# Another split of a weight load over the DMA engines in a decode block (attention with a KV cache beside a gMLP)

## The chip, the cores and the metric

One Trainium2 chip, one core of it. The metric is the device time of one execution of the kernel in microseconds (us), as the median of several runs. Beside it there is one execution under the hardware profiler; its time and its span are given below, and all durations in this document come from such profiled executions.

## The reference

Four tokens (batch B = 4, one position each, D = 640) go through a layernorm and then through two blocks whose results are added to the input.

```python
xn = _layernorm(x)
# A: attention of one query against a cache, H = 32 heads, Sk = 4096 keys, Dh = 128
q = (xn @ wq)                                   # 640 x 4096
scores = einsum('bhqd,bhkd->bhqk', q, k_cache) * Dh ** -0.5
p = softmax(scores);  o = einsum('bhqk,bhkd->bhqd', p, v_cache);  A = o @ wo
# B: gMLP, Fh = 864
z = gelu(xn @ w_in)                             # 640 x 1728
z1, z2 = z[..., :Fh], _layernorm(z[..., Fh:])
g = w_sp * z2 + b_sp                            # one position, so w_sp is 1 x 1
B = (z1 * g) @ w_out                            # w_out is 864 x 640
return x + A + B
```

Everything is bf16. The caches are 4 x 32 x 4096 x 128 each, 134 MB of K and 134 MB of V; `wq` and `wo` have 5.2 MB each, `w_in` 2.2 MB, `w_out` 1.1 MB (864 rows of 1280 bytes).

## The kernel before

**Loads.** Nearly all bytes are fetched by SyncE's queue (SP) in one fixed order: `wq` (L119), `w_in` (L122), the first 384 rows of `w_out` (L126, L127), two pieces of its other rows (`load_piece`, L139 and L140), then the cache in units of 8 heads of one batch entry, each 128 partitions x 65,536 bytes (`load_unit`, L174 to L181): K of the four batch entries of head group 0, then V and K in turn, last V of the last group. `wo` comes in four parts of 1280 KB (`load_wo`, L187): one after the last K unit of the second group, and three behind everything else (L570 to L572), the last of them cut into five transfers so that the products with it can start before all of it is there. The cache units lie in one buffer `kv` of five half-unit slots; a unit's load waits until the slot's former reader is done, so SP always has one or two units in the queue ahead of the one in use.

**`w_out`.** The product with `w_out` contracts over its 864 rows in chunks of up to 128 (one row per partition). The first nf = 384 rows are the common rows: `FA` = 3 chunks over all 128 partitions, in `kv`. Two transfers bring them, 256 rows as two rows per partition (L126) and 128 rows as one per partition (L127). The other 480 rows lie in `FR` = 17 further chunks in `w_words`, which fill only some partitions; L128 sets that part of `w_words` to zero first. The table `PC` (L61) says how. An entry `(p0, p1, n, k)` puts n rows into each of the partitions p0 to p1; `load_piece` writes the DRAM side with k as the slowest dimension. The three entries move 20 x 10, 12 x 12 and 8 x 17 rows. The first two are issued on SP, the third on GpSimd (POOL), after a small load `walk` of 14 short rows (L141) on the same queue.

```python
FA = 3
FR = 17
PC = ((0, 20, 10, 5), (32, 44, 12, 3), (60, 68, 17, 2))
```

**gMLP.** `z_ps` (L338, L339) gets the products of xn with the columns of `w_in` that belong to the common rows: per contraction chunk (5) and partition group (4) one matmul for two of the three chunks and one for the third, since the rows of the two transfers lie differently. `zr_ps` (L343) gets the others, one matmul for each partition group that an entry of `PC` touches. ScalarE applies GELU (L349, L357, L360); layernorm and gating run on GpSimd and VectorE over 128 x 32*(FA+FR) elements (L371 to L390); then (FA+FR) x 2 products with `w_out` add to `proj` (L403).

**Attention.** Per K unit eight steps `emit_K`: a 32x32-block transpose on VectorE (L425) and eight matmuls (L436). After a group's four K units a softmax, then four V units (`emit_V`, L509). After the last V unit: selection matmul (L531), `oT` (L534 to L543), the products with the last parts of `wo` (`emit_proj` L555, then L599 to L614), one add (L617) and two output transfers (L620).

Of the kernel before, what the change touches and what calls it, by code (L numbers as in the profile page):

```python
# [16 lines left out]
def kernel(  # L17
# [19 lines left out]
    nc = tc.nc  # L37
    P = 128
# [3 lines left out]
    DC = D // P  # L42
# [9 lines left out]
    NG = H // HG  # L52
# [2 lines left out]
    F2 = B_w_in.shape[1]  # L55
    Fh = F2 // 2
    FA = 3
    FR = 17
    nf = FA * P

    PC = ((0, 20, 10, 5), (32, 44, 12, 3), (60, 68, 17, 2))  # L61
    f_at = [nf]
    for p0, p1, n, _ in PC:
        f_at.append(f_at[-1] + (p1 - p0) * n)
    assert Fh == f_at[-1]
    FC = FA + FR
    NOUT = A_wo.shape[1]
# [18 lines left out]
    def misc_ps(shape, dtype):  # L86
        misc_ctr[0] += 1
        return ps_m.tile(shape, dtype, tag="misc", name=f"misc{misc_ctr[0]}")
# [5 lines left out]
    n_p = (2 * TC + 1) * 16  # L94
    w_words = const.tile([P, max(2 * NKT + n_p, FR * NOUT // 2)], F32, name="w_words")
    kT_t = w_words[:, 0:2 * NKT].rearrange("p (i n) -> p i n", i=2)
    pT_t = w_words[:, 2 * NKT:2 * NKT + n_p].bitcast(BF16).rearrange("p (j r) -> p j r", r=32)

    def at_slot(i, n, off=0):
        return kv[:, i * SL + off:i * SL + off + n]  # L100
# [22 lines left out]

    w_out = at_slot(2, FA * NOUT, n_in).rearrange("p (c n) -> p c n", c=FA)

    nc.sync.dma_start(out=w_out[:, 0:2], in_=B_w_out[0:2 * P, :].rearrange("(p c) n -> p c n", p=P))  # L126
    nc.sync.dma_start(out=w_out[:, 2:3], in_=B_w_out[2 * P:nf, :].rearrange("(p c) n -> p c n", p=P))  # L127
    nc.vector.memset(w_words[:, 0:FR * NOUT // 2], 0.0)  # L128
    w_rest = w_words[:, 0:FR * NOUT // 2].bitcast(BF16).rearrange("p (c n) -> p c n", c=FR)

    def load_piece(eng, t):
        p0, p1, n, k = PC[t]
        return eng.dma_start(out=w_rest[p0:p1, 0:n].rearrange("p c n -> p (c n)"),
                             in_=B_w_out[f_at[t]:f_at[t + 1], :].rearrange("(r i c) n -> i r (c n)", i=k, c=n))
# [39 lines left out]
    def load_unit(item):  # L174
        key, u = item
        g, b = divmod(u, B)
        cache = A_k_cache if key == "k" else A_v_cache
        src = cache[b, g * HG:(g + 1) * HG].rearrange("e (m t) d -> (e m) (t d)", t=T)
        c = cuts.get(item, (0, T))
        for t0, t1 in zip(c[:-1], c[1:]):  # L180
            nc.sync.dma_start(out=unit(item, t0, t1), in_=src[:, t0 * Dh:t1 * Dh])  # L181
# [5 lines left out]
    def load_wo(g, c_cuts=(0, HG)):  # L187
        for c0, c1 in zip(c_cuts[:-1], c_cuts[1:]):
            nc.sync.dma_start(out=wo_t[g][:, c0:c1, :], in_=wo_q[g][:, c0:c1, :])  # L189
# [30 lines left out]
    xnT = const.tile([P, DC, 32], BF16)  # L220
# [43 lines left out]
    for q in range(4):  # L264
        nc.gpsimd.tensor_copy(out=SelE[32 * q:32 * q + 32, :, q % 2, :],
                              in_=b8[32 * q:32 * q + 32, 8:8 + HP, None].to_broadcast((32, HP, P // HG)))
# [10 lines left out]
                          in_=ident_f[:].rearrange("p (q x c) -> p q x c", q=2, c=C2))  # L277
# [12 lines left out]
    for hf in range(NH):  # L290
        nc.tensor.matmul(proj[0:32, 0:NO2], lhsT=ident_bf[:XR, 1 - hf:33 - hf],
                         rhs=x_bf[:, hf * NO2:(hf + 1) * NO2], start=(hf == 0), stop=False)
# [4 lines left out]
    for hf in range(2):  # L297
        for c in range(DC):
            for j in range(NG):
                n0 = j * HG * Dh + hf * 512  # L300
                nc.tensor.matmul(q4_ps[32 * j:32 * j + 32, hf * 512:hf * 512 + 512], lhsT=xnT[:, c, :],  # L301
                                 rhs=wq[:, c, n0:n0 + 512], start=(c == 0), stop=(c == DC - 1))
# [14 lines left out]
    w_z = w_in.rearrange("p c (a f) -> p c a f", a=2)  # L317
    z_ps = misc_ps([P, 2, FA, 32], F32)
# [3 lines left out]
    z_in = [[], [], [], []]  # L322
    for t, (p0, p1, n, k) in enumerate(PC):
        src = w_z[:, :, :, f_at[t]:f_at[t + 1]]
        for q in range(p0 // 32, (p1 - 1) // 32 + 1):
# [5 lines left out]
                src_q = src  # L331
            z_in[q].append((t, x0 - 32 * q, x1 - 32 * q, src_q))
    z_of = [[sum((x1 - x0) * PC[t][2] for t, x0, x1, _ in z[:m]) for m in range(len(z) + 1)] for z in z_in]
    w_z2 = w_z[:, :, :, 0:2 * P].rearrange("p c a (q j i) -> p c q a i j", q=4, j=32)
    w_z1 = w_z[:, :, :, 2 * P:nf].rearrange("p c a (q j) -> p c q a j", q=4)
    for c in range(DC):
        for q in range(4):
            nc.tensor.matmul(z_ps[32 * q:32 * q + 32, :, 0:2], lhsT=xnT[:, c, :], rhs=w_z2[:, c, q], start=(c == 0), stop=False)  # L338
            nc.tensor.matmul(z_ps[32 * q:32 * q + 32, :, 2], lhsT=xnT[:, c, :], rhs=w_z1[:, c, q], start=False,  # L339
                             stop=(c == DC - 1))  # L340
        for q in range(4):
            for m, (_, _, _, src) in enumerate(z_in[q]):
                nc.tensor.matmul(zr_ps[32 * q:32 * q + 32, :, z_of[q][m]:z_of[q][m + 1]], lhsT=xnT[:, c, :], rhs=src[:, c],  # L343
                                 start=(c == 0 and m == 0), stop=(c == DC - 1 and m == len(z_in[q]) - 1))
# [5 lines left out]
    for q in range(4):  # L350
        rows = slice(32 * q, 32 * q + 32)
        for m, (t, x0, x1, _) in enumerate(z_in[q]):
            p0, p1, n, k = PC[t]
            z = zr_ps[rows, :, z_of[q][m]:z_of[q][m + 1]]
# [3 lines left out]
            else:  # L358
                for a in range(2):
                    nc.scalar.activation(out=dst[:, a].rearrange("p c (i r) -> p c i r", i=k),  # L360
                                         in_=z[:, a].rearrange("p (r i c) -> p c i r", i=k, c=n), func=ACT.Gelu_apprx_tanh)
# [36 lines left out]
    for f0 in range(0, FC, 4):  # L398
        for hf in range(NH):
            for fc in range(f0, min(f0 + 4, FC)):  # L400
# [3 lines left out]
                                 rhs=(w_out[:, fc] if fc < FA else w_rest[:, fc - FA])[:, hf * NO2:(hf + 1) * NO2],  # L404
                                 start=(fc == 1 and hf == 0), stop=False)
# [11 lines left out]
    def emit_K(u, k):  # L417

        g, b = divmod(u, B)
        hh = first.get(u, 0) ^ (k // 4)  # L420
        qp, kh = k // 2 % 2, k % 2
        t0 = 2 * TC * (2 * hh + qp)
        kw = unit(("k", u), t0, t0 + 2 * TC).bitcast(F32).rearrange("p (t w) -> p t w", w=KW)[:, :, 32 * kh:32 * kh + 32]
        kT = kT_t[:, k % 2]
        nc.vector.transpose(kT.rearrange("p (t r) -> p t r", r=32), kw)  # L425
        if ("S", g) not in state:
            S_new = ps_s.tile([P, 2, TC, M], F32, tag="S", name="S")
            state[("S", g)] = S_new
        S_ps = state[("S", g)]
        kb = kT.bitcast(BF16).rearrange("p (i t e m w) -> p i t e m w", i=2, e=NE, m=M, w=2)  # L430
        w0 = 8 - (b * C2 + hh)
        for w in range(2):
            for i in range(2):
                for e in range(NE):
                    q = 2 * qp + e
                    nc.tensor.matmul(S_ps[32 * q:32 * q + 32, i], lhsT=QZ[:, b, 2 * kh + w, e, w0:w0 + 32],  # L436
                                     rhs=kb[:, i, :, e, :, w], start=(b == 0 and k < 4 and kh == 0 and w == 0),
                                     stop=(b == B - 1 and k >= 4 and kh == 1 and w == 1))
# [89 lines left out]
    def emit_sel(g):  # L528

        ox = misc_ps([P, B, P // HG, HG], F32)  # L530
        nc.tensor.matmul(ox[:].rearrange("p b q c -> p (b q c)"), lhsT=SelX[:].rearrange("p h q -> p (h q)"),  # L531
                         rhs=state["R"][:].rearrange("p b d -> p (b d)"), start=True, stop=True)
        om = ppool.tile([P, B, P // HG, HG], F32, tag="p", name="om")
        nc.vector.tensor_tensor(out=om[:], in0=ox[:], in1=MkQ[:, None, :, None].to_broadcast((P, B, P // HG, HG)), op=ALU.mult)  # L534
        state[("om", g)] = om
# [19 lines left out]
    def emit_proj(g, h2=range(2), close=False):  # L555
        for h in h2:
            for hf in range(NH):
                for c in range(4 * h, 4 * h + 4):
                    o_mul(proj[32 * (c % 2):32 * (c % 2) + 32], g, c, hf, hf * NO2, (hf + 1) * NO2, False,
                          close and c == HG - 1 and hf == NH - 1)  # L560

    fill_qz(0)
    for i, item in enumerate(seq):
        if i + 1 < len(seq):
            key, u = seq[i + 1]
            load_unit(seq[i + 1])
            if key == "k" and u == 2 * B - 1:
                load_wo(u // B - 1)
        else:
            load_wo(NG - 3)  # L570
            load_wo(NG - 2)
            load_wo(NG - 1, (0, 2, 4, 6, 7, 8))  # L572
        key, u = item
        g, b = divmod(u, B)
        if key == "k":
            done = b == B - 1 and g > 0
            for k in range(8):
                emit_K(u, k)
                if done and k == 1:
                    emit_sel(g - 1)  # L580
                if done and k == 2:
                    emit_oT(g - 1)
                if done and k == 5 and g == 1:
                    emit_proj(g - 1)
            if b == B - 1:
                if g < NG - 1:
                    fill_qz(g + 1)
                softmax(g)
        else:
            emit_V(u)  # L590
# [58 lines left out]
```

## Time and profile before

| | us |
|---|---|
| median of 3 runs (lowest to highest) | 663.54 (663.45 to 664.74) |
| the profiled execution's own time | 663.36 |
| its span, first to last instruction | 661.6 |
| VectorE busy | 377.3 (57%) |
| TensorE busy | 281.7 (43%) |
| ScalarE, GpSimd busy | 73.9, 70.3 |
| bytes moved | 282.60 MB, 427 GB/s over the span |

How to read it: the page gives busy time by engine, DMA queues by packets and bytes, the chain of work that ended last and the costliest groups of instructions. The view by windows gives, for each stretch of time, the busy time of each engine and the DMA share, which is the mean busy share of the core's 16 DMA engines. The trace behind it holds, for every DMA packet, its queue, start, duration and size, and, for every transfer, the moments at which its 16 shares landed (one semaphore step each). From these, times are quoted as "landings", in us from the start of the span.

### The profile page before, as it was taken

What the parts mean: (1) busy time and instruction counts of PE and PEld (TensorE: products, weight loads), DVE (VectorE), ACT (ScalarE), POOL (GpSimd) and SP (SyncE); (2) the same over time, 40 slices, a digit from 0 to 9 for tenths busy, and PEclk for the clock granted to TensorE, in tenths of its full rate; (3) what the DMA queues carried; (4) which work ended last, traced back from release to release, by engine and by line L of the source; (5) the groups of instructions that cost most, each with busy time, mean ns of one, the idle gap of its engine ahead of it and who ended that gap; (6) DMA issues with size and microseconds to landing.
All of it is one profiled execution on the core that took longest, in us unless ns stands there. A gap on an engine that the chain in (4) does not pass through costs nothing.

```text
span 661.6 us, 5513 instructions
## 1 busy us (share of the span) xinstructions
PE 281.7 (43%) x2293; PEld 106.9 (16%) x2293; DVE 377.3 (57%) x307; ACT 73.9 (11%) x143; POOL 70.3 (11%) x138
## 2 busy tenths in 40 slices
PE   0445555437052455334435075532606245652236
PEld 0221111112011121111112021110202112120012
DVE  4329989766191758718346196864629175971112
ACT  0300000330100000340200000070110000043200
POOL 3620000030200000130300000030020000003300
PEclk9868879778687697677759677875867778666779
DMA  8999999999999999999999999999999999999997
GB/s 367 458 421 440 425 436 445 436 421 440 421 436 437 444 405 436 441 441 436 433 420 428 437 422 445 442 425 432 432 433 432 433 440 411 446 432 429 423 423 286
DMA packets 7276, 282.60 MB, mean 427 GB/s; under 512 B 929, under 2 KB 1324, under 8 KB 1836
## 3 DMA queue, kind: packets, MB, share of 16 engines
q1 hardware_dynamic: 7112, 282.07, 98.9%
q8 instruction: 18, 0.29, 0.2%
q0 software_dynamic: 112, 0.18, 0.1%
q14 instruction: 6, 0.05, 0.0%
q10 hardware_dynamic: 28, 0.01, 0.0%
HBM read 282.25 MB, written 0.01 MB: 427 GB/s over the span
## 4 chain that ended last, share of the span: by engine, by line
DMA 74%; DVE 12%; issue 11%; PE 2%; ACT 0%; SPq 0%; DVEq 0%; ACTq 0%
DMA kv<-in_A_k_cache_dram 63%; DVE w_words L425 11%; DMA kv<-in_A_v_cache_dram 5%; DMA kv<-in_A_wo_dram 3%; DMA kv<-in_A_wq_dram 3%; PE O L509 1%; DVE w_words L491 0%; PE S L436 0%; DVE Zb L469 0%; DVE m L443 0%; PE last L552 0%; ACT p_bf L485 0%; SPq L189 0%; PE proj L552 0%; PE misc L447 0%
## 5 line engine op out<-in xcount | busy, mean ns | idle before, releaser
L425 DVE STREAM_TRANSPOSE w_words<-kv 128x2048 f32<-128x2048 f32 x128 | 282.8, 2275 | 127.2 <-DMA kv<-in_A_k_cache_dram 127.2
L436 PE MATMUL S<-w_words,QZ 128*32 128x512 bf16 x1024 | 183.3, 490 | 262.5 <-DVE w_words L425 262.5
L436 PEld LDWEIGHTS <-QZ 128*32 128x32 bf16 x1024 | 59.2, 110 | 384.3 <-issue 318.1
L509 PE MATMUL O<-kv,Zb 128*32 128x512 bf16 x1024 | 72.0, 443 | 57.6 <-DMA kv<-in_A_v_cache_dram 51.1
L473 ACT ACTIVATE Zb<-w_words,MkE 32x128 bf16<-32x128 bf16 x120 | 60.9, 508 | 117.2 <-PE O L509 103.3
L518 DVE TENSOR_TENSOR om<-O,Mk 128x512 f32<-128x512 f32 x15 | 10.4, 692 | 92.1 <-PE O L509 92.1
L471 POOL TENSOR_SCALAR Zb<-w_words,MkE 32x128 bf16<-32x128 bf16 x60 | 43.3, 722 | 138.6 <-PE O L509 118.0
L485 ACT ACTIVATE p_bf<-S,negmax 128x1024 bf16<-128x1024 f32 x4 | 4.5, 1114 | 401.5 <-DVE negmax L453 401.5
L509 PEld LDWEIGHTS <-Zb 128*32 128x32 bf16 x1024 | 33.3, 110 | 96.1 <-issue 66.5
L469 DVE TENSOR_SCALAR Zb<-w_words,MkE 32x128 bf16<-32x128 bf16 x76 | 24.9, 327 | 2.3
L411 POOL COPY QZ<-qT 32x32 bf16<-32x32 bf16 x16 | 5.0, 315 | 184.9 <-PE S L436 184.3
L519 DVE TENSOR_REDUCE R<-om 128x128 f32<-128x512 f32 x15 | 15.3, 1020 | 0.5
L496 POOL TENSOR_SCALAR rs<-MkB,rowsum 128x4 f32<-128x4 f32 x4 | 1.2, 296 | 112.2 <-ACT p_bf L485 112.2
L491 DVE STREAM_TRANSPOSE w_words<-p_bf 128x1024 bf16<-128x1024 bf16 (+1 forms) x8 | 9.6, 1240 | 5.9 <-ACT p_bf L485 4.1
L542 POOL MEMSET oT<- 128x66 bf16 x4 | 0.5, 146 | 98.0 <-PE proj L552 98.0
L443 DVE TENSOR_REDUCE m<-S 128x1 f32<-128x1024 f32 x4 | 4.9, 1224 | 6.1 <-PE S L436 6.1
L521 DVE TENSOR_SCALAR R<-O,Mk 128x128 f32<-128x128 f32 x1 | 0.4, 351 | 13.0 <-PE O L509 13.0
L531 PE MATMUL misc<-R,SelX 128*128 128x512 f32 x8 | 4.5, 644 | 7.2 <-DVE R L519 5.5
L301 PE MATMUL q<-kv,xnT 128*32 128x512 bf16 x40 | 4.5, 631 | 6.4 <-DVE xnT L222 6.4
L498 PE MATMUL misc<-rs,SelE 128*128 128x4 f32 x8 | 2.3, 364 | 10.4 <-POOL rs L496 10.4
L552 PE MATMUL proj<-kv,oT 128*8 128x320 bf16 x52 | 5.6, 352 | 1.2 <-DMA kv<-in_A_wo_dram 1.2
L128 DVE MEMSET w_words<- 128x5440 f32 x1 | 4.6, 4592 | 1.9 <-issue 1.9
(107 smaller groups left out, 87.9 us busy)
## 6 DMA issues: line engine op xcount, KB each, us to landing
kv<-in_A_k_cache_dram SPq DMA_DIRECT2D x8, 4096.0 KB, 30.2
kv<-in_A_v_cache_dram SPq DMA_DIRECT2D x1, 6144.0 KB, 28.6
kv<-in_A_wq_dram SPq DMA_DIRECT2D x1, 5120.0 KB, 17.2
kv<-in_A_wo_dram SPq DMA_DIRECT2D x3, 1280.0 KB
kv<-in_B_w_in_dram SPq DMA_DIRECT2D x1, 2160.0 KB, 22.7
kv<-in_A_v_cache_dram SPq DMA_DIRECT2D x1, 2048.0 KB
kv<-in_A_wo_dram SPq DMA_DIRECT2D x3, 320.0 KB, 22.7
kv<-in_B_w_out_dram SPq DMA_DIRECT2D x1, 320.0 KB, 23.0
```

Source lines behind the costliest of these rows:

```text
L411: nc.gpsimd.tensor_copy(out=QZ[r0:r0 + 32, :, :, :, 8 + 8 * hp], in_=qT[32 * g:32 * g + 32, NE * hp:NE * hp + NE].rearrange("p e a b -> p ...
L425: nc.vector.transpose(kT.rearrange("p (t r) -> p t r", r=32), kw)
L436: nc.tensor.matmul(S_ps[32 * q:32 * q + 32, i], lhsT=QZ[:, b, 2 * kh + w, e, w0:w0 + 32], rhs=kb[:, i, :, e, :, w], start=(b == 0 and k < ...
L443: nc.vector.tensor_reduce(out=m1[:], in_=S_ps[:].rearrange("p i t m -> p (i t m)"), axis=AX.X, op=ALU.max)
L469: nc.vector.tensor_scalar(out=dst, in0=src, scalar1=mk, scalar2=None, op0=ALU.mult)
L471: nc.gpsimd.tensor_scalar(out=dst, in0=src, scalar1=mk, scalar2=None, op0=ALU.mult)
L473: nc.scalar.activation(out=dst, in_=src, func=ACT.Copy, scale=mk)
L491: nc.vector.transpose(pT_t[:, j0:j1, :], blocks)
L509: nc.tensor.matmul(O_ps[32 * q:32 * q + 32, :, :], lhsT=Zb[b % 2][:, w].rearrange("p h c -> p (h c)"), rhs=vv[:, w * 4 * Dh:(w + 1) * 4 * ...
L518: nc.vector.tensor_tensor(out=om4[:], in0=O_ps[:], in1=Mk4[:, :, None].to_broadcast((P, 4, Dh)), op=ALU.mult)
L519: nc.vector.tensor_reduce(out=R, in_=om4[:].rearrange("p c d -> p d c"), axis=AX.X, op=ALU.add)
L552: nc.tensor.matmul(dst[0:nb, 0:n1 - n0], lhsT=state[("oT", g)][:, c0:c0 + nb], rhs=wo_t[g][:, c, n0:n1], start=start, stop=stop)
```

## The change

The rows of `w_out` are dealt out anew. The 384 common rows come in one transfer, three rows to each partition, in place of two transfers. The 480 other rows lie in 15 chunks in place of 17: 20 partitions x 9 rows, 20 x 9 and 8 x 15. The matmuls of `z` for the common rows become one per contraction chunk and partition group. Apart from that, the third part of `wo` (`load_wo(NG - 2)`) is cut into two transfers of 640 KB.

```diff
-    FR = 17
+    FR = 15
     nf = FA * P
 
-    PC = ((0, 20, 10, 5), (32, 44, 12, 3), (60, 68, 17, 2))
+    PC = ((0, 20, 9, 5), (32, 52, 9, 5), (60, 68, 15, 2))
...
-    nc.sync.dma_start(out=w_out[:, 0:2], in_=B_w_out[0:2 * P, :].rearrange("(p c) n -> p c n", p=P))
-    nc.sync.dma_start(out=w_out[:, 2:3], in_=B_w_out[2 * P:nf, :].rearrange("(p c) n -> p c n", p=P))
+    nc.sync.dma_start(out=w_out, in_=B_w_out[0:nf, :].rearrange("(p c) n -> p c n", p=P))
...
-    w_z2 = w_z[:, :, :, 0:2 * P].rearrange("p c a (q j i) -> p c q a i j", q=4, j=32)
-    w_z1 = w_z[:, :, :, 2 * P:nf].rearrange("p c a (q j) -> p c q a j", q=4)
+    w_za = w_z[:, :, :, 0:nf].rearrange("p c a (q j i) -> p c q a i j", q=4, j=32)
     for c in range(DC):
         for q in range(4):
-            nc.tensor.matmul(z_ps[32 * q:32 * q + 32, :, 0:2], lhsT=xnT[:, c, :], rhs=w_z2[:, c, q], start=(c == 0), stop=False)
-            nc.tensor.matmul(z_ps[32 * q:32 * q + 32, :, 2], lhsT=xnT[:, c, :], rhs=w_z1[:, c, q], start=False,
-                             stop=(c == DC - 1))
+            nc.tensor.matmul(z_ps[32 * q:32 * q + 32], lhsT=xnT[:, c, :], rhs=w_za[:, c, q], start=(c == 0), stop=(c == DC - 1))
...
             load_wo(NG - 3)
-            load_wo(NG - 2)
+            load_wo(NG - 2, (0, 4, 8))
             load_wo(NG - 1, (0, 2, 4, 6, 7, 8))
```

In the order of the instructions, the change takes 40 TensorE instructions out of the `z` products and 8 out of the products with `w_out`, one transfer out of SP's list at the start and adds one to it near the end. VectorE, ScalarE and GpSimd keep their number of instructions; those over 640 (5440) elements per partition go over 576 (4800).

## The prediction

> **What bounds the kernel now.** I read the queues and the slices first. The 16 DMA engines are busy in every slice, and nearly all packets are on one queue.
>
> ```profile
> DMA  8999999999999999999999999999999999999997
> ...
> q1 hardware_dynamic: 7112, 282.07, 98.9%
> q8 instruction: 18, 0.29, 0.2%
> q0 software_dynamic: 112, 0.18, 0.1%
> q14 instruction: 6, 0.05, 0.0%
> ```
>
> So no single wait sets the end; the sum of packets does, on the engine that has most. The two "instruction" queues fetch program code through the same engines: 18 packets of 16 KB and six of 8 KB within the span. They matter below.
>
> Next I read the last stretch of the chain of waits.
>
> ```profile
> 633.82 23.04 DMA kv<-in_A_wo_dram
> 656.86 0.04 issue
> 656.91 0.23 PE last L552
> 657.14 0.64 PE proj L552 x4
> 657.78 0.68 PE last L552 x15
> 658.46 0.04 issue
> 658.50 0.32 PE last L552 x4
> 658.82 0.02 issue
> 658.85 0.32 DVE o_bf L617
> ```
>
> The last four matmuls start at 658.50, 0.04 us after the last landing of `wo` (658.46), and TensorE was idle before them. From there a fixed 3.1 us follow (matmuls, add, output transfer) to 661.6. The span is therefore: the last landing on the slowest engine, plus 3.1.
>
> Last, the view by windows, DMA share in the last but one column.
>
> ```profile
> 652.00:655.00 3.00, 2.08 (x18) 0.79 (x18) 1.97 (x3) 0.00 (x0) 0.00 (x0) 1.00 0.97 390
> 655.00:656.50 1.50, 1.19 (x16) 0.76 (x16) 0.00 (x0) 0.00 (x0) 0.00 (x0) 1.00 0.88 328
> 656.50:657.50 1.00, 0.66 (x9) 0.36 (x7) 0.48 (x1) 0.00 (x0) 0.00 (x0) 1.00 0.36 127
> 657.50:658.50 1.00, 0.96 (x21) 0.73 (x17) 0.61 (x2) 0.00 (x0) 0.00 (x0) 1.00 0.11 36
> ```
>
> The engines do not finish together: 0.97 busy, then 0.36, then 0.11. A share that is moved off the last ones is gained; a share put on them is lost, us for us. So the question is which engines are last, and what the new split does to them.
>
> **Who is last.** The page doesn't name the engines, but the 16 landings of every transfer do it indirectly: an engine works through its queue in order, at a constant pace (a 65,536-byte packet takes 2.418 us in nearly all cases), so its distance from the earliest engine changes only where it gets something extra. Sorted distances, in us:
>
> ```
> transfer (earliest landing)   distance of the 16 landings from the earliest
> first K unit (40.60)   0 .13 .14 .17 .29 .32 .36 1.47 1.65 | 2.23 2.28 | 3.62 3.76 | 4.50 4.81 4.92
> K half (89.01)         0 .14 .18 .19 .33 .37 1.44 1.66 1.80 | 2.27 3.21 | 3.62 3.77 | 4.49 4.81 4.92
> V unit (471.06)        0 .09 .22 .28 .43 .82 1.73 1.75 1.89 1.96 2.13 2.28 3.34 3.46 3.69 3.70
> last of wo (654.91)    0 1.43 1.59 1.64 1.66 1.76 1.89 1.91 2.01 2.16 3.12 3.13 3.32 3.37 3.51 3.55
> ```
>
> The groups of the first row follow from the pieces of `w_out`. Piece 1 lands on five engines at 23.23, 23.46, 23.48, 23.50, 23.78; piece 2 on three at 25.50, 25.75, 26.07. Four packets of 15,360 bytes take 4 x 573 ns = 2.29 us, and 23.23, 23.46 and 23.78 plus 2.29 are just these three. So the three of piece 2 are among the five of piece 1 (distances 4.5 to 4.9: the **heavy three**), and the other two of the five are at 2.23 and 2.28 (the **light two**). GpSimd's piece sits on two more (3.62, 3.76).
>
> The Trainium skill, page "DMA: Bandwidth & Descriptors", section "Why a DMA increments its semaphore by 16 and not by 1", says that a transfer from SP over k engines takes the lowest-numbered k. The landings just read agree. By it, the changed second piece, now with k = 5, falls on the very same five.
>
> Now the code fetches. At 88.3 us there is an 8 KB code packet (0.32 us). In the next landings one of the light two has gone from 2.27 to 3.21, +0.94: the engine loses more than the packet's own time. The same engine, call it **X**, gains 0.94 again at 279 (3.22 to 4.16, corrected for the earliest engine, which itself moves by 1.43 on a 16 KB packet at 288) and 0.96 at 469 (2.73 to 3.69). X thus pays about 2.85 us for code. One of the heavy three pays 0.67 at 35 and 0.68 at 279, the other light one 0.67 at 614. The 16 KB packets, some 1.5 us each, go round eight other engines in turn. At the end X, which had the small share, stands beside the heavy three at the top (3.69 and 3.70 at 471).
>
> **The change, part by part.**
>
> 1. *Pieces.* A packet of 9 rows (11,520 bytes) should take 479 - 1280 x 0.0367 = 432 ns (479 ns for 12,800 and 573 for 15,360 bytes give 0.0367 ns a byte). Two pieces of four packets and a 9 ns semaphore packet each: 3.47 us on each of the five. Heavy three before: 4 x 479 + 4 x 573 + 18 ns = 4.23, now **-0.75**. Light two before: 4 x 479 + 9 ns = 1.93, now **+1.55**. GpSimd's two: packets of 19,200 for 21,760 bytes, 4 x 94 ns = -0.38.
> 2. *Common rows.* 8 x (102 + 55) + 18 ns = 1.27 before; 8 packets of 3840 bytes at 102 + 47 = 149 ns and one semaphore, 1.20: -0.07 on all engines.
> 3. *Third part of `wo` in two.* 8 x 385 ns become 16 x 196 (102 + 94), +0.06 and a semaphore: +0.07 on all. Parts 2 and 3 cancel. An earlier start of the products with it gains nothing: the last landing, not TensorE's backlog, starts the last four matmuls.
> 4. *Compute.* L128 shrinks by 12% of 4.59 us (-0.54), TensorE loses 24 matmuls (20 of 0.19 us, overlapped, four of about 0.13), GpSimd's three long steps 10% of 2.5 + 0.9 + 1.5 us. All of it ends by 43.6 us, and the next thing, the first transpose, starts at 45.74 after 7.1 us of waiting for the first K unit. Cost: nothing. If that cover were gone, the gain would be some 1.5 us of compute, but only in front of a stream of loads that has to arrive anyway.
> 5. *Queues.* SP's list loses L127 (0.92 us), but SP waits there for L128 until 6.55. One issue more near the end costs 0.4 us at 633, 15 us and more ahead of the data. As a transfer waits for a semaphore to come free, now the last two of `wo` wait for landings of the last V unit (644.2 and 649.1, later by what X adds); the first engine reaches the last one at 654.5, and the first `wq` packet started 1.0 us after its issue. Covered by about 3 us. The nearest approach elsewhere is the third K unit, issued at 54.76 with the engines busy till 59.95. No idle engine arises.
> 6. *Code.* TensorE has 48 instructions fewer, so its 16 KB packets come a little later, on engines that aren't last (the third round costs at most 1.5 us on one that stands at 1.9 or less). VectorE, ScalarE and GpSimd keep their counts, so I take the 8 KB fetches as unchanged in time, place and cost.
>
> **Sum.** At the last landing X is the one at 3.51 or 3.55; with +1.55 it stands at 5.06 to 5.10 from an earliest engine that stays at 654.91. The heavy three drop to 2.6 to 2.8. The last landing moves from 658.46 to 659.99, +1.5 us, and everything behind it with it. From the profiled execution's 663.36 that is 664.9; the median of the runs shown is 0.18 above that execution. I predict **665.0**, +0.22%. X's packets could take 0.1 less or more each way, as distances shrank by 0.15 over the small packets at the end: 664.6 to 665.3.
>
> The Trainium skill, page "Runtime: NRT & Kernel Launch", section "Instruction fetch mechanics", calls instruction fetch hidden behind the pace at which instructions are issued. For the engines that run the instructions no wait here contradicts it; for the loads the trace does (some 0.95 three times on X). If the rule held for the loads too, the five would carry nothing else and this change would level them.
>
> **Rivals.**
>
> - *X's code goes elsewhere (not slower).* Fetch engines could be laid out anew for the changed program. If none of the two hit hardest is among the light two, these end at 1.43 + 1.55 = 3.0, the heavy three at 2.8, and the last is the engine at 3.13 after its third 16 KB packet: 3.55 - 3.13, -0.4 us, **663.1**. X itself would then stand at 3.53 - 2.85 + 1.55 = 2.2. The break-even lies where X pays 2.85 - 1.53 = 1.3 us for code in place of 2.85: one fetch, not three. For: the placement is seen in one execution only. Against: the instruction counts that drive the 8 KB fetches don't change. The same 663.1 would come if the second piece fell on five other engines. Chance 0.25.
> - *More code on X.* A fourth 8 KB fetch (they came 190 us apart; the next would be near 659) slips in ahead of the end: +0.95, **666.0**. Against: VectorE's counts are the same. Chance 0.07.
> - *Part of X's tail is free.* Alone at the end, X might run faster than the constant pace, or something else is already as late as X: half of 1.5 is lost, **664.2**. Against: small packets take 55 ns and 385 ns in the crowd and near the end. Chance 0.08.
>
> **Chances.** Forecast 0.60, rivals 0.25, 0.07, 0.08. About 0.2%, 1.3 us, is what a measurement can tell from no change here, so 664.87 is the bound. The forecast lies just over it; I give it 0.8 to come out there (0.48), and with the second rival 0.55 for slower. Same: 0.12 + 0.08 + 0.22 = 0.42. Faster by over 1.3 us would need the last landing below a distance of 2.2, where several engines stand that the change doesn't touch: 0.03. The range takes in the first and nearly the second rival: 662.9 to 666.0.
>
> **What would show it.** Right: the last landing near 660.0, the latest alone for about 1.5 us; the DMA share near 0.06 between 658.5 and 659.5; in the first K unit distances of about 3.8 (two), 3.7 to 4.2 (three) in place of 2.25 and 4.5 to 4.9, and one of the two stepping up by 0.95 at 88, 279 and 469. Wrong: the steps fall on another group, or a K or V load starts with an idle engine before it.

## The result and the profile after

| | before | changed |
|---|---|---|
| median of 16 runs (lowest to highest), us | 663.39 (663.25 to 664.74) | 664.78 (664.56 to 664.98) |
| profiled execution, span, us | 661.6 | 662.9 |

The medians lie 1.39 us (0.21%) apart; the ratio over all runs is 1.0019, 95% interval 1.0011 to 1.0026. So the changed kernel is slower, clear of the measurement, and stands right at the 0.2% that the prediction had set as a bound: just over it by the medians, just under it by the ratio. Two of the 16 runs of the kernel before (664.42 and 664.74; beside e1 to e4 below, 11 of 33) came out about 1 us above the rest, which pulls the ratio down and not the medians; no trace here shows why. (663.39 is the median over 16 runs of the kernel before; the prediction knew three.)

The queues on the page of the changed kernel hold the same bytes in sum as before (0.02 MB went from q0, GpSimd's piece, to q1), in ten packets more on q1, and the same code packets:

```profile
q1 hardware_dynamic: 7122, 282.09, 98.7%
q8 instruction: 18, 0.29, 0.2%
q0 software_dynamic: 112, 0.16, 0.1%
q14 instruction: 6, 0.05, 0.0%
```

The end of the chain of waits, changed kernel:

```profile
618.48 31.92 DMA kv<-in_A_v_cache_dram
650.40 0.02 issue
650.42 9.39 DMA kv<-in_A_wo_dram
659.81 0.04 issue
659.85 0.32 PE last L548 x4
660.17 0.02 issue
660.20 0.32 DVE o_bf L613
```

Again the last four matmuls start 0.04 us after the last landing, now at 659.81 in place of 658.46, and again 3.1 us follow. The chain goes through the issue at 650.4, which waited for a semaphore of the last V load; that wait sets nothing, since the earliest engine came to that transfer only at 654.4. The view by windows of the changed kernel shows who is late (DMA share in the last but one column):

```profile
656.50:657.50 1.00, 0.71 (x8) 0.28 (x7) 0.05 (x2) 0.00 (x0) 0.00 (x0) 1.00 0.29 109
657.50:658.50 1.00, 0.48 (x7) 0.46 (x8) 0.47 (x1) 0.00 (x0) 0.00 (x0) 1.00 0.10 38
658.50:659.50 1.00, 0.97 (x19) 0.66 (x18) 0.62 (x2) 0.00 (x0) 0.00 (x0) 1.00 0.06 20
659.50:660.50 1.00, 0.57 (x8) 0.20 (x7) 0.30 (x1) 0.00 (x0) 0.00 (x0) 1.00 0.06 16
```

0.06 is one engine of 16. From 658.5 on a single engine works, and everything waits for it. In the last window part of the share is that engine's last 0.3 us and a code packet. The landings, read as in the prediction:

```
changed kernel, earliest landing   distance of the 16 landings from the earliest
first K unit (40.62)   0 .01 .03 .05 .20 .27 .39 .48 1.24 | 3.11 3.24 | 3.57 3.60 3.73 3.96 4.14
K half (89.04)         0 .04 .06 .19 .27 .49 1.25 1.54 1.93 | 3.09 3.24 | 3.60 3.71 3.95 4.16 4.51
V unit (470.89)        0 .26 .35 .51 .57 1.83 1.86 1.93 2.00 2.23 2.32 2.36 2.67 2.92 3.14 5.22
last of wo (654.80)    0 1.73 1.75 1.82 1.83 1.83 1.89 1.97 2.06 2.24 2.51 2.77 2.85 3.00 3.64 5.01
```

The five engines with 72 rows start together at 3.57 to 4.14. One of them, X, steps from 3.57 to 4.51 at the 8 KB code packet near 89.7 us, again by 0.95 near 279 and from 4.23 to 5.22 at 472. At the end it is alone at 5.01; the next one stands at 3.64.

### The profile page after: what moved, and what is told of

Its sections match the earlier page's. It is cut to its first block, busy times and chain, and to the rows that moved or that the text cites. A ratio compares the mean times of both kernels' runs of the same rounds, so it can differ in the third digit from the quotient of the medians.

```text
span 662.9 us, 5465 instructions
## 1 busy us (share of the span) xinstructions
PE 285.2 (43%) x2269; PEld 108.3 (16%) x2269; DVE 376.7 (57%) x307; ACT 73.9 (11%) x143; POOL 69.2 (10%) x138
## 4 chain that ended last, share of the span: by engine, by line
DMA 76%; DVE 12%; issue 11%; PE 1%; SPq 0%; DVEq 0%
DMA kv<-in_A_k_cache_dram 65%; DVE w_words L421 11%; DMA kv<-in_A_v_cache_dram 9%; DMA kv<-in_A_wo_dram 1%; PE O L505 1%; DVE w_words L127 1%; SPq L132 0%; DVEq L421 0%; SPq L180 0%; PE last L548 0%; DVE o_bf L613 0%
## 5 line engine op out<-in xcount | busy, mean ns | idle before, releaser
L505 PE MATMUL O<-kv,Zb 128*32 128x512 bf16 x1024 | 75.1, 459 | 58.7 <-DMA kv<-in_A_v_cache_dram 40.6
L530 DVE TENSOR_TENSOR om<-misc,h 128x512 f32<-128x512 f32 x4 | 2.8, 691 | 4.9 <-PE misc L527 4.9
```

The source lines that it names most:

```text
L505: nc.tensor.matmul(O_ps[32 * q:32 * q + 32, :, :], lhsT=Zb[b % 2][:, w].rearrange("p h c -> p (h c)"), rhs=vv[:, w * 4 * Dh:(w + 1) * 4 * ...
```

## The experiments

The theory: the end is X's last landing, X is one engine, and it is late because it gets the same rows as four others and VectorE's code besides. All times below are medians; each group was run beside the kernel before on the same chip (663.31 to 663.38).

**The piece table alone, both ways.** `e1_old_pieces` is the changed kernel with

```diff
-    PC = ((0, 20, 9, 5), (32, 52, 9, 5), (60, 68, 15, 2))   # FR = 15
+    PC = ((0, 20, 10, 5), (32, 44, 12, 3), (60, 68, 17, 2)) # FR = 17
```

> The changed kernel with the piece table of before (20 x 10, 12 x 12, 8 x 17 rows, 17 chunks); the common rows stay in one transfer and the third part of wo in two. Theory (the share on engine X sets the end): X has 40 rows again, the last landing goes back by 1.4 to 1.5 us, time 663.3 to 663.5, ratio to before 0.999 to 1.000. Rival (the merged transfer, the cut of wo or the z products cost the time): it stays at 664.6 to 664.9, ratio 1.002.

Measured 663.40, ratio 0.9997 (0.9988 to 1.0006). `e2_new_pieces` is the kernel before with the opposite edit.

> The kernel before with the piece table of the change alone (20 x 9, 20 x 9, 8 x 15 rows, 15 chunks); common rows in two transfers, wo uncut. Theory: X has 72 rows, stands alone 1.4 us behind the next at the end; 664.7 to 665.0, ratio 1.002. Rival (the cost is in the other edits): 663.3 to 663.5, ratio 1.000.

Measured 664.85, ratio 1.0018 (1.0009 to 1.0027). The end of the chain of waits in e1:

```profile
649.39 9.44 DMA kv<-in_A_wo_dram
658.83 0.04 issue
658.87 0.32 PE last L548 x4
```

So the piece table brings the whole loss. The merged transfer of the common rows, the cut in `wo` and the fewer `z` products together change nothing that can be measured.

**Which of the five X is.** `e3_four_engines` gives four engines 80 rows and the fifth 40; `e4_four_engines_less` gives them 76 and 32.

```diff
+    PC = ((0, 20, 10, 5), (32, 48, 10, 4), (60, 68, 15, 2))  # e3, FR = 15
+    PC = ((0, 20, 8, 5), (32, 48, 11, 4), (60, 68, 18, 2))   # e4, FR = 18
```

> The changed kernel with 20 x 10, 16 x 10 (k = 4) and 8 x 15 rows: four engines get 80 rows, the fifth of the five 40. It asks which of the five X is. If X is the fifth: X is back at its 40 rows (distance of the last landing 3.5), the other light one goes to 3.35, the heavy three to 3.0 to 3.2; 663.3 to 663.5, ratio 0.999 to 1.000, though each of four engines has 8 rows more than in the change. If X is the fourth: X at 3.53 + 1.92 = 5.45, 665.1 to 665.4, ratio 1.003. Rival that the engine with most rows is last, wherever code goes (72 in the change, 80 here, 88 before): time between the two, nearer to before only if more rows on four engines were good, which it can't explain.

> The changed kernel with 20 x 8, 16 x 11 (k = 4) and 8 x 18 rows, 18 chunks: four engines get 76 rows, the fifth of the five 32, GpSimd's two 72. If X is the fifth: X at 3.15, heavy three 2.8 to 3.0, the other light one 3.15, GpSimd's two 2.3, one engine with three 16 KB code packets at 3.1: all level, the last landing 0.4 us ahead of before, 662.9 to 663.2, ratio 0.999 to 1.000: a little faster than both kernels. If X is the fourth: X at 5.3, 664.9 to 665.2, ratio 1.0025.

Measured 665.17, ratio 1.0024 (1.0015 to 1.0033), and 664.99, ratio 1.0019 (1.0011 to 1.0028): both what was forecast for X as the fourth. In e3 the last landing of X is at 660.17, alone:

```profile
658.50:659.50 1.00, 0.93 (x16) 0.66 (x16) 0.41 (x2) 0.00 (x0) 0.00 (x0) 1.00 0.06 23
```

In its landings the engine with 40 rows stays at 2.0 from 60 to 118 us, while one of the four steps from 3.99 to 4.95 at 90 us. The hope that e4 would beat both kernels fell with the fifth place. That the four of piece 2 lie among the five of piece 1 fits what the Trainium skill says in "DMA: Bandwidth & Descriptors", section "Why a DMA increments its semaphore by 16 and not by 1": the lowest-numbered k. The rival by which the engine with most rows is last fails: before, three engines have 88 rows, more than any engine here, and that kernel is faster than e3 and e4.

**Is it the code?** `e5_vector_code` adds eight small instructions after each of the 16 V units' reductions; the scheduler put them early, between 11 and 36 us.

```diff
+    junk = const.tile([P, 1], F32, name="junk")
...
+        for _ in range(8):
+            nc.vector.memset(junk[:], 0.0)
```

`e6_scalar_code` has `nc.scalar.copy(out=junk[:], in_=eps_t[:])` in their place.

> The changed kernel plus 128 writes of one column of ones' place on VectorE (memset of a 128 x 1 tile that nobody reads), most of them before the first K unit, where VectorE waits. They add 8 KB of code to VectorE's stream and no data. Theory (X carries VectorE's code): one more 8 KB fetch, X steps up four times in place of three, its last distance goes from 5.0 to 5.9 to 6.0; time +0.9 to +1.0 against the change: 665.6 to 665.9, ratio to before 1.0035. Rival (code of VectorE does not go through the engine that ends last, or a fetch costs loads nothing): 664.6 to 664.9, ratio 1.002.

> The changed kernel plus 128 one-column copies on ScalarE (result read by nobody): the same 8 KB of code, in another engine's stream. Theory (each stream has its own load engine; ScalarE's is not X): another engine steps up by 0.7 to 1.0 once more and ends at most at a distance of 4.6, behind X; time unchanged, 664.6 to 664.9, ratio 1.002. Rival (any code costs the same at the end, or extra small instructions do): 665.6 to 665.9 as with VectorE's.

Measured 665.70 (ratio 1.0035, 1.0021 to 1.0049) and 664.82 (1.0018, 1.0010 to 1.0027). Both fetch one 8 KB code packet more (at 20.8 us in e5, at 29.2 in e6). This row is the same on both pages, with 0.06 MB in place of 0.05:

```profile
q14 instruction: 7, 0.06, 0.0%
```

The added instructions take 7.6 us on VectorE and 24.4 us on ScalarE (group view, first e5, then e6):

```profile
L523 DVE MEMSET junk<- 128x1 f32 x128 | 7.6, 59 | 7.6
```

```profile
L523 ACT COPY junk<-eps_t 128x1 f32<-128x1 f32 x128 | 24.4, 191 | 7.6 <-POOL eps_t L200 3.7
```

The cheaper ones cost the kernel 0.92 us, the dearer ones nothing. The time they ran in is not the cause either: in e5 the transfer behind was issued at 31.3 in place of 25.7, still 9 us before an engine was free for it. What moved is the end, in e5:

```profile
651.32 9.42 DMA kv<-in_A_wo_dram
660.74 0.04 issue
660.78 0.32 PE last L551 x4
```

660.74 is 0.93 after the changed kernel's 659.81. In the landings of e5 the last engine stands at 4.42 already at 60 us, 5.40 after 90 us, and 6.23 at the end, the next at 3.85; in e6 the last is at 5.23 and the next at 3.75. So VectorE's code comes in through X, and 8 KB more of it moved the end by 0.93 us while X was last.

**A third share on GpSimd: a miss.** To relieve X and the heavy three, `e7_third_share` puts part of the rows on a third engine of GpSimd's piece, and `e8_third_share_shifted` in addition shifts the small load ahead of it.

```diff
+    PC = ((0, 20, 6, 5), (32, 44, 14, 3), (64, 76, 16, 3))   # e7 and e8, FR = 16
...
+    walk = const.tile([12, NST], BF16)                       # e8: 12 rows, i = 6
```

> The changed kernel with 20 x 6, 12 x 14 (k = 3) and 12 x 16 rows (GpSimd, k = 3), 16 chunks: X and the other light one get 24 rows, the heavy three 80, three engines of GpSimd's piece 64. One engine was earliest in all runs so far, 1.2 to 2 us ahead of the next; if GpSimd's third share falls on it, it goes to 3.1, X to 2.8, the heavy three to 3.0 to 3.2: all but level, the last landing 0.4 us before that of the kernel before, 662.9 to 663.2, ratio 0.999 to 1.000: faster than both. If the third share falls on an engine that fetches TensorE's code, that one stands at 4.6 to 5.0 and is last: 664.4 to 664.8, ratio 1.0015 to 1.002, with X no longer last in either case. Rival (rows do not set the end): 664.6 to 664.9 with X last.

> The same pieces, with the small load ahead of them on GpSimd's queue over 6 rows pairs in place of 7 (12 rows of 512 bytes, k = 6; nobody reads it). If GpSimd's shares go on from where its last transfer stopped, all three move down by one engine. One of this run and the one before it should then have the earliest engine among its three: 662.9 to 663.2 there, 664.4 to 664.8 in the other. If both are slow, the earliest engine is not a neighbour of GpSimd's two.

Measured 668.77 (ratio 1.0075, 1.0061 to 1.0089) and 667.89 (1.0066, 1.0053 to 1.0078), far outside. X was not last in either, as expected; but the first K unit came on the earliest engine at 42.27 and 43.53 in place of 40.6, so that all 16 engines had lost time. The packets of GpSimd's piece, 0.76 us at best, took up to 1.53 and 1.58. In e7 one engine ends alone on top of that, 7.13 from the earliest with the next at 3.35; it stands at 5.8 after the first K unit and steps by some 1.55 at two 16 KB packets (198 and 485 us) and at no 8 KB packet, so it is one that fetches TensorE's code, as in the slower of the two forecasts. I had changed two things, the number of shares and the partitions they are written to (64 to 76 in place of 60 to 68). `e10_moved_piece` changes the second alone (five matmuls of the `z` products go with it, as the piece then touches one partition group in place of two):

```diff
-    PC = ((0, 20, 9, 5), (32, 52, 9, 5), (60, 68, 15, 2))
+    PC = ((0, 20, 9, 5), (32, 52, 9, 5), (64, 72, 15, 2))
```

> The changed kernel with GpSimd's piece of 8 x 15 rows in partitions 64 to 72 in place of 60 to 68; nothing else. In the two runs with three shares on GpSimd, the loads of all engines fell behind by 1.1 to 1.7 us while that piece was moved (packets of 20,480 bytes took 0.76 to 1.53 us), which no theory had foreseen. If the placement did it (the two engines write into partitions that other engines write at the same time), this run is slower than the change by 0.5 to 2 us, 665.3 to 667, with packets of 19,200 bytes above 0.714 us. If the third share did it, this run is as the change: 664.6 to 664.9, packets at 0.714 us.

Measured 665.19, ratio 1.0029 (1.0018 to 1.0041): a shade less than expected, and its interval meets that of the change, so the time alone doesn't decide. The packets do: eight of 0.714 us in the change, 0.714 to 1.318 here (median near 0.92), with the first K unit at 41.27 in place of 40.62. One engine stands at 6.66 there, the next at 3.98, and is last at the end (5.09, X behind it at 4.85). The view by windows, first the changed kernel, then e10 (GB/s in the last column):

```profile
14.00:20.00 6.00, 1.73 (x20) 0.83 (x24) 3.07 (x7) 0.29 (x1) 5.41 (x20) 1.00 0.90 386
```

```profile
14.00:20.00 6.00, 0.00 (x0) 0.10 (x1) 2.88 (x7) 0.29 (x1) 5.41 (x20) 1.00 0.89 358
```

From 14 to 20 us the engines are as busy (0.89 for 0.90) and move less (358 for 386 GB/s): the placement of a piece slows the loads around it. The Trainium skill, "DMA: Bandwidth & Descriptors", section "The descriptor swizzle", gives each engine its own partitions in a transfer to all 128, 60 to 63 to engine 7 and 64 to 67 to engine 8. If GpSimd's two shares run on 7 and 8, the old place is their own and the new one their neighbours'. The trace doesn't name the engines, so this reading fits but isn't shown; nor is it shown how much of the loss of e7 and e8 is due to the third share.

**A share for a sixth engine.** `e9_six_engines` lowers X to 32 rows and the heavy three to 80 by spreading piece 1 over six engines.

```diff
+    PC = ((0, 24, 8, 6), (32, 44, 12, 3), (60, 68, 18, 2))   # FR = 18
```

> The changed kernel with 24 x 8 rows over six engines (k = 6), 12 x 12 over three and 8 x 18 on GpSimd's two, 18 chunks: X 32 rows, the heavy three 80, GpSimd's two 72, a sixth engine 32. If the sixth is the one that was earliest in all runs, it goes to 1.5, X to 3.15, the heavy three to 3.0 to 3.2, the engine with three 16 KB code packets stays at 3.1: the last landing 0.3 to 0.5 us before that of the kernel before, 662.9 to 663.2, ratio 0.9990 to 0.9998, the fastest of all. If the sixth fetches TensorE's code, it goes to 3.5 or, with a third packet, 4.6: 663.3 to 664.4, ratio 1.000 to 1.0015. Rival (rows on X don't set the end): 664.6 to 664.9.

Measured 663.30, ratio 0.9998 (0.9989 to 1.0007): 1.5 us faster than the change, the same as before, so the sixth is not the idle one.

```profile
657.50:658.50 1.00, 0.81 (x15) 0.49 (x15) 0.41 (x2) 0.00 (x0) 0.00 (x0) 1.00 0.12 38
658.50:659.50 1.00, 0.26 (x4) 0.04 (x3) 0.32 (x1) 0.00 (x0) 0.00 (x0) 1.00 0.00 0
```

The last landing is 658.41, against 658.46 before. Several engines end within 0.4 us of the last, at 3.5 to 3.85 from an earliest one that still has nothing to do. No version here beats the kernel before by more than the measurement can tell.

## Why the prediction was right, point by point

- *X and its code* (forecast): right in place, size and mechanism. X stepped at 89.7, 279 and 472 us by 0.94 to 0.99; e1 and e2 put the loss on the piece table, e5 and e6 on VectorE's code.
- *Pieces, +1.55 on the light two, -0.75 on the heavy three*: the new packets take 432 ns and GpSimd's 714, both as worked out (432; 808 less 94). In the first K unit the five stand at 3.57 to 4.14, where I had written 3.7 to 4.2 and 3.8; the order at the start differs by some 0.2 between executions.
- *Sum*: the last landing was put at 659.99 and is 659.81, so +1.35 in place of +1.53. The difference is there from the start: in the first K unit X lands at 44.2 us (40.62 + 3.57), where the light two landed at 42.83 and 42.88 before, so +1.3 in place of +1.55, and this lead stays to the end. X's packets have the 432 ns of the estimate; by the order of the landings its first piece came some 0.2 sooner than worked out (23.05 for 23.2), which is of the size by which the order at the start differs between executions. *Common rows* and *cut of `wo`* were worked out at -0.07 and +0.07: the new packets have the 149 ns of the estimate, and 200 ns for 196, so they don't explain it.
- *Median*: 665.0 against 664.78. Part of the 0.22 is the base: the median of three runs, 663.54, is 663.39 over sixteen. Which side of the bound it came out on was close to chance: the medians' +1.39 lies just over 1.33 us, the ratio of 1.0019 just under 0.2%, and the interval takes in both. I had given 0.42 to "same" and 0.55 to "slower".
- *Compute costs nothing*: in the change the last step of the gating, the transpose at 36.96, came 0.8 us sooner, and VectorE then waited 7.2 us for the first K unit. That covers it, as argued.
- *Queues*: SP's last two issues moved to 645.5 and 650.4, both waits forecast, 8 and 4 us ahead of the earliest engine. No cost.
- *TensorE's code*: the last 16 KB packet moved from 655.9 to 659.9, onto an engine that was done.
- *Rivals*: code laid out anew (0.25), a fourth fetch (0.07) and a free tail (0.08) did not occur; e5 shows that the second would have cost what it was priced at (0.95 against 0.92).

## What to carry to other kernels

Where the DMA engines are busy throughout, as here, the end is the sum of the engine with the most work, and an even split of bytes is not an even split of work: program code arrives through the same engines, and the engine that brings it should get fewer rows (X with 72 rows cost 1.4 us against 40). The landings of the 16 shares, sorted and followed from transfer to transfer, show this without any engine's name. A test costs little: add code that does nothing to one engine's stream and see whether the end moves.

## What the runs showed of the hardware that was not expected

- A code packet costs the loads more than its own time: 0.32 us of packet moves an engine's later landings by 0.66 to 0.99 us, and a 16 KB packet of 1.0 to 1.1 us by some 1.5. What fills the difference isn't shown.
- GpSimd's piece moved by four partitions took packets of up to 1.32 us for 0.714 and slowed loads of other engines with it (e10).
- The distances between the engines persist: in the kernel before, the heavy three stand at 4.50, 4.81 and 4.92 after the first K unit and at 4.48, 4.79 and 4.94 some 213 us later. In these traces the larger changes come where an engine fetches code; over the small transfers at the end the distances shrink by 0.1 to 0.2.
